# One planned order of a gated linear attention and token/channel mixer kernel against another: block 0's keys on VectorE, the rest planned anew

## The chip, the core and the metric

The kernel runs on one core of a Trainium2 chip, as one program. Five engines take instructions from queues of their own, each strictly in order: PE (TensorE, matrix products), DVE (VectorE), ACT (ScalarE), POOL (GpSimd) and SP (SyncE, which here only issues DMA transfers). They meet through semaphores. An instruction that is not ready holds up everything behind it on its engine. The metric is the device time of one execution in microseconds (us), the median of three runs; lower is better.

## What is computed

Two stages in a row. For each of 4 batches and 8 heads, a recurrence over 768 steps with a decaying 48 x 48 state; its output, as 768 x 384, goes through a mixer over tokens and then one over channels:

```python
# attention: q, k, v, alpha are (4, 8, 768, 48)
for t in range(768):
    state = alpha[:, :, t, :, None] * state + einsum('bhd,bhe->bhde', k[:, :, t], v[:, :, t])
    y[:, :, t] = einsum('bhd,bhde->bhe', q[:, :, t], state)
x = y.transpose(0, 2, 1, 3).reshape(4, 768, 384)
# mixer
h = maximum(x.transpose(0, 2, 1) @ w_tok1, 0) @ w_tok2      # 768 -> 256 -> 768
u = x + h.transpose(0, 2, 1)
out = u + maximum(u @ w_ch1, 0) @ w_ch2                     # 384 -> 1536 -> 384
```

Inputs and output are float32; the kernel multiplies in bfloat16.

## The kernel before

The sequence of each batch is cut into three chunks of 256 steps. Chunk n (0 to 11) belongs to batch n // 3. The 256 steps lie as 128 partitions x 2 slots, and the halves (hf 0 and 1) of a chunk are handled one after the other. The steps of a chunk, with the names that the program gives them (n behind the name):

- `ld_at`, `ld_qt`, `ld_kt`, `ld_vt`: loads of alpha, q, k, v, 384 KB each, issued from SP's queue or ACT's.
- `ln` (ACT, L598) takes the logarithm of alpha; `cumw` (PE, L604) sums it along the sequence; `E`, `Et`, `IE` (ACT, L637, L641) give the factor, the total and the inverse factor. From chunk 3 on a shorter form is used: `P`, `ln1`, `lnP` (L592, L595), `r`, `cum`, and `k0a`, `q0r` ahead of the scalings.
- `qq`/`ql` and `kk`/`kl` (L653): queries times E, keys times IE, one instruction for each slot in chunks 0 to 4; `vb` converts the values (L697 on ACT, L698 on DVE or POOL).
- `trq`/`trk` (PE, L666) transpose both, `evq`/`evk` copy the result out of PSUM. From chunk 6 on a DMA transpose does this (`dq`, `dk`, `pq`).
- `G` (PE): products of queries and keys; `mask` (DVE, L720) keeps the causal part. `K` (PE): products of keys and values; `s`, `sa`, `sm` make the new states; `vs`, `ka`, `kb`, `kc` are copies between partition halves.
- `ia`/`ib` and `y` (PE) give the output of a half, `x` copies it out.

The mixer of batch b has `t1` (PE, L805; chunk half kc of output block m) and its relu `ht`, `t2` (PE, L810) and the sum `u` (DVE, L814), the transposes `up` with copies `ut`, then `c1` (PE, L829: `c1_b_mc_half`, three products each) with its relu `rt` on ACT (L800) or DVE (L802), and `c2` (PE, L834) with `o` (DVE, L838) and the stores `st`. The weights are loaded in pieces (`ldw_wt10` and so on) and converted (`cw_...`). Mixer b runs on PE interleaved with the attention of batch b + 1.

Ahead of batch 0 there are fillers: `f1_...` and `f3_...` are one or three products of a tile of zeros (128 x 512) into a bank that the named step uses later. They compute nothing that is used. 28 such products are issued.

Nothing schedules this at run time. `build` (from L117) declares all steps with the engines that they may use. Three strings hold the plan: `ORDER` lists all 947 steps in the order of issue, each with a letter for its engine (t PE, s ACT, v DVE, g POOL, y SP); `BUFS` gives the buffer of each tile at its first use, PSUM banks among them; `GATES`, empty here, could tie transfers together. `run` reads them, and the last loop emits the steps one by one, so the order within an engine is the order in the string. The wait of a step comes from what it reads and from the former users of its buffers. One wait is added on top: `shared` (L684) makes steps with `port=True` (scalings, conversions, half copies on DVE and POOL) wait for the one before them in the list when that ran on the other of the two engines.

PSUM has 8 banks. A `c1` needs one until its `rt` has run; a `cumw`, a `K` or a `G` needs a pair.

Of the kernel before, what the change touches and what calls it, by code (L numbers as in the profile page):

```python
# [378 lines left out]
G0_0t sm1_0v f3_trq1t G1_0t K1t P3g ld_kt2y ld_vt2y lnP3s trk1t trq1t sa0_1t evk1s evq1s ld_kt3y qq2g mask0_0v  # L379
mask1_0v ldw_wt10y ld_vt3y sm0_1v cum3t y0_0t x0_0s ib0t sa1_1t f3_trq2t ld_at4y ld_qt3y ql2v trq2t sm1_1v kl2v E3s  # L380
IE3s kk2g vs0_1g ldw_wt11s y1_0t evq2v G0_1t ia1t kk3g f1_G11t ldw_wt20y ldw_wt21y mask0_1v k0a3g x1_0s G1_1t ld_kt4y
vb2s trk2t mask1_1v ldw_wc10y r13s ib1t K2t evk2s sa0_2t sm0_2v G0_2t cw_wt10s mask0_2v kl3g ldw_wc11y vs1_1g vs0_2g
vs1_2s ka3s vb3s f3_G12t G1_2t kb3s ldw_wc13y t1_0_1_0t y0_1t trk3t ld_at5y y1_1t cw_wt11g ib2t ia2t ln14s mask1_2v
y0_2t x0_1v x0_2v x1_1s vs1_3s vs0_3s ld_qt4s ldw_wc12y kc3g t1_0_1_1t y1_2t t1_0_0_0t t1_0_1_2t P4g t1_0_0_1t
t1_0_0_2t t1_0_0_3t t1_0_0_4t q0r3g x1_2v t1_0_0_5t t1_0_1_3t evk3v qq3g t1_0_1_4t ql3g lnP4s t1_0_1_5t k0a4g ht_0_0s
cw_wt20s K3t ht_0_1v cum4t cw_wt21s t2_0_0t t2_0_1t IE4s s0_3v sa1_3v u_0_0v t2_0_2t kk4g ldw_wc15y trq3t u_0_1v
u_0_2v t2_0_3t t2_0_5t kl4g E4s evq3s up_0_0t t2_0_4t u_0_3v cw_wc10s u_0_5v u_0_4v up_0_1t ut_0_1s ut_0_0v ld_vt4y
G1_3t G0_3t up_0_2t ib3t mask0_3v mask1_3v trk4t ldw_wc14y c1_0_0_0t c1_0_1_0t cw_wc11g ut_0_2s c1_0_2_0t c1_0_3_1t
r14s cw_wc13s ldw_wc21y c1_0_7_1t evk4s y1_3t y0_3t rt_0_1_0v q0r4v ka4v qq4v ql4g x0_3s x1_3v rt_0_0_0v rt_0_2_0v P5g
cw_wc15g c1_0_7_0t c1_0_6_1t rt_0_7_0s rt_0_7_1s cw_wc12s rt_0_3_1s c1_0_0_1t ld_qt5y c1_0_6_0t trq4t c1_0_2_1t  # L390
c1_0_4_1t ld_kt5y ldw_wc22y sm1_3g cw_wc14g vb4g lnP5s c1_0_10_1t evq4s ldw_wc20s rt_0_0_1s rt_0_6_0v rt_0_6_1v
ld_vt5s rt_0_2_1s c1_0_11_1t c1_0_11_0t rt_0_10_1v cum5t rt_0_11_1v G0_4t G1_4t kb4s IE5s rt_0_4_1v cw_wc21g kc4g
ln15s E5s c1_0_10_0t c1_0_3_0t r15s rt_0_10_0s c1_0_9_1t vs1_4g ldw_wc23y mask0_4v rt_0_9_1s rt_0_11_0s mask1_4v
ldw_wc24y c1_0_8_0t c1_0_4_0t c1_0_8_1t ia4t q0r5v vs0_4s y0_4t rt_0_8_0s rt_0_4_0s c1_0_1_1t c1_0_5_0t K4t c1_0_9_0t
ldw_wc25s rt_0_5_0s qq5v rt_0_8_1s x0_4s rt_0_9_0s cw_wc22s rt_0_3_0v rt_0_1_1v trq5t c1_0_5_1t ld_at6y k0a5g sa0_4v
# [36 lines left out]
c2_2_2_2t c2_2_1_1t t2_3_3t c2_2_2_3t o_2_3v u_3_5v c2_2_1_2t c2_2_1_3t u_3_4v o_2_4v u_3_3v c2_2_0_2t o_2_2v ux_3_1y
c1_3_7_0t c1_3_0_0t c1_3_4_0t c1_3_10_0t c1_3_5_0t c2_2_0_3t c1_3_2_0t rt_3_4_0s st_2_4s st_2_2y rt_3_5_0s rt_3_2_0s
# [459 lines left out]
```

## Time and profile before

| | us |
|---|---|
| median of three runs (lowest to highest) | 165.89 (165.33 to 166.85) |
| the profiled execution: its time | 165.84 |
| its span, first to last instruction | 164.1 |
| instructions in the span | 4068 |
| mean granted TensorE clock | 0.99 |

A row of the timeline has the start, the busy time, the engine, the line, the operation, the tiles written and read, their shapes and a count; in square brackets stands how long the engine had been idle before it and what ended that. A row of a group has the total busy time, the mean ns of one, and the idle time before the group with its releasers. PE is matrix products, PEld the loads of their stationary operand, which overlap. A matmul's end is modelled and includes its drain, so single durations are longer than the distance from one to the next. Engine names with q (ACTq, SPq) are issues of transfers.

### The profile page before, as it was taken

The numbers are of one execution on the slowest core, as the hardware profiler recorded it, in microseconds if no ns is written. First come the engines' busy times: TensorE is split into PE (matmuls) and PEld (weight loads), VectorE is DVE, ScalarE is ACT, GpSimd is POOL, SyncE is SP. The second block draws the span as 40 slices with busy tenths as digits, with TensorE's granted clock in tenths as the row PEclk, the third lists the DMA queues.
The fourth block names the chain that finished last, engine by engine and source line by source line (L and its number), as shares of the span: only waits on it lengthen the run. The fifth ranks groups of instructions, "written<-read, shape, count | busy, mean of one in ns | idle before, by whom it ended". The sixth has DMA issues, their size and how long they took to land.

```text
span 164.1 us, 4068 instructions
## 1 busy us (share of the span) xinstructions
PE 155.5 (95%) x1601; PEld 98.2 (60%) x1601; DVE 110.8 (68%) x197; ACT 101.1 (62%) x188; POOL 75.5 (46%) x94
## 2 busy tenths in 40 slices
PE   7959889899999999999999999999999999999992
PEld 2444656576657676665667666666566665566660
DVE  4056999689699777967789998874591283524341
ACT  3698798998998786289995947466615101562000
POOL 4054489972942827289795494739700000000000
PEclk9995999999999999999999999999999999999999
DMA  4999999999999998999999999699012135220314
GB/s 127 324 318 321 248 340 279 348 348 344 342 363 336 291 265 202 249 302 211 239 239 174 234 184 221 144 221 248 19 48 100 48 68 129 90 98 9 113 71 143
DMA packets 76322, 34.46 MB, mean 210 GB/s; under 512 B 68112, under 2 KB 76304, under 8 KB 76304
## 3 DMA queue, kind: packets, MB, share of 16 engines
q1 hardware_dynamic: 64704, 27.73, 66.5%
q10 hardware_dynamic: 11600, 6.49, 13.7%
q8 instruction: 12, 0.20, 0.5%
q14 instruction: 6, 0.05, 0.1%
HBM read 25.17 MB, written 4.72 MB: 182 GB/s over the span
## 4 chain that ended last, share of the span: by engine, by line
PE 52%; DVE 4%; ACT 2%; ACTq 1%; issue 1%
PE ps L834 22%; PE ps L829 19%; PE ps L604 6%; PE ps L805 3%; PE ps L810 2%; DVE u L814 1%; ACTq L545 1%; DVE o L838 1%; DVE pkk L653 1%; DVE ut L698 1%; ACT vb L697 0%; ACT ut L697 0%; DVE rt L802 0%; DVE ss L762 0%; ACT lf L592 0%
## 5 line engine op out<-in xcount | busy, mean ns | idle before, releaser
L834 PE MATMUL ps<-wc,rt 128*128 128x384 bf16 (+2 forms) x300 | 54.7, 320 | 0.0
L829 PE MATMUL ps<-ut,wc 128*128 128x384 bf16 x288 | 51.8, 326 | 0.3 <-ACT E L631 0.2
L800 ACT ACTIVATE rt<-ps 128x384 bf16<-128x384 f32 x55 | 25.3, 493 | 24.6 <-PE ps L829 24.5
L829 PEld LDWEIGHTS <-wc 128*128 128x128 bf16 x288 | 27.0, 98 | 17.7 <-issue 1.2
L834 PEld LDWEIGHTS <-rt 128*128 128x128 bf16 x300 | 27.6, 98 | 16.6
L802 DVE TENSOR_SCALAR rt<-ps 128x384 bf16<-128x384 f32 x41 | 21.6, 552 | 14.4 <-PE ps L829 13.9
L720 DVE TENSOR_TENSOR gtm<-ps,mk 128x1024 bf16<-128x1024 f32 x24 | 28.3, 1217 | 2.7 <-PE ps L604 2.5
L653 POOL TENSOR_TENSOR pkk<-in,IE 128x384 bf16<-128x384 f32 (+1 forms) x12 | 14.3, 1206 | 9.4 <-DVE pkq L653 6.3
L838 DVE TENSOR_TENSOR o<-ps,u 128x384 f32<-128x384 f32 (+2 forms) x25 | 13.3, 535 | 6.1 <-PE ps L834 6.0
L814 DVE TENSOR_TENSOR u<-ps,x 128x384 bf16<-128x384 f32 x24 | 12.3, 552 | 4.6 <-PE ps L810 4.5
L653 POOL TENSOR_TENSOR pkq<-in,E 128x384 bf16<-128x384 f32 (+1 forms) x8 | 11.2, 1408 | 7.0 <-DMA in<-in_moe_w_ch_dram 3.8
L697 ACT CAST x<-ps 128x384 bf16<-128x384 f32 x19 | 9.0, 481 | 7.7 <-PE ps L604 7.7
L697 ACT CAST vb<-in 64x384 bf16<-64x384 f32 (+1 forms) x18 | 11.8, 658 | 2.4 <-DMA in<-in_v_dram 1.6
L698 POOL CAST vb<-in 64x384 bf16<-64x384 f32 (+1 forms) x17 | 9.5, 559 | 7.0 <-issue 3.2
L805 PE MATMUL ps<-x,wt 128*128 128x384 bf16 x48 | 11.4, 326 | 0.3 <-ACT x L697 0.3
L604 PE MATMUL ps<-zs 128*128 128x512 bf16 x28 | 9.9, 495 | 1.1 <-DVE zs L507 1.1
L810 PE MATMUL ps<-ht,wt 128*128 128x384 bf16 x48 | 10.1, 326 | 0.7 <-ACT wt L697 0.7
L589 POOL TENSOR_TENSOR in<-in 128x384 f32<-128x384 f32 x9 | 9.0, 1000 | 3.4 <-DMA in<-in_alpha_dram 2.5
L653 DVE TENSOR_TENSOR pkq<-in,E 128x384 bf16<-128x384 f32 (+1 forms) x9 | 6.0, 689 | 6.5 <-ACT E L637 4.6
L645 POOL TENSOR_TENSOR in<-in,in 128x384 f32<-128x384 f32 x7 | 7.0, 1001 | 5.4 <-DVE in L649 3.0
L768 DVE TENSOR_TENSOR tmp<-ps,ss 128x384 f32<-128x384 f32 x12 | 6.6, 554 | 3.5 <-POOL ss L771 1.8
L604 PE MATMUL ps<-tpq,tpk 48*64 48x128 bf16 (+1 forms) x288 | 8.3, 221 | 0.3 <-ACT tpk L697 0.2
(93 smaller groups left out, 212.2 us busy)
## 6 DMA issues: line engine op xcount, KB each, us to landing
in<-in_alpha_dram SPq DMA_DIRECT2D x11, 384.0 KB, 6.3
in<-in_q_dram SPq DMA_DIRECT2D x10, 384.0 KB, 5.2
in<-in_moe_w_ch_dram SPq DMA_DIRECT2D x10, 384.0 KB, 7.3
in<-in_k_dram SPq DMA_DIRECT2D x9, 384.0 KB, 5.8
in<-in_v_dram SPq DMA_DIRECT2D x9, 384.0 KB, 6.0
out_dram<-o SPq DMA_DIRECT2D x14, 192.0 KB, 2.4
out_dram<-o ACTq DMA_DIRECT2D x9, 192.0 KB, 1.9
in<-in_moe_w_tok_dram SPq DMA_DIRECT2D x3, 384.0 KB, 5.6
```

Source lines behind the costliest of these rows:

```text
L604: return self.pe.matmul(out, lhsT=lhsT, rhs=rhs, start=start, stop=stop, skip_group_check=True)
L653: self.shared(self.eng[e].tensor_tensor(self.t(dst)[:, c : c + z, :, 0:D], self.t(src)[:, :, c : c + z, :].rearrange("p h s d -> p s h d") ...
L697: return self.act.copy(d, s)
L720: self.nc.vector.tensor_tensor(self.t(gtm)[:, hf, :, :], self.pair(gp).rearrange("p a (j t) -> p (a j) t", t=128), bass.AP(tensor=m.tensor ...
L800: self.act.activation(d, s, AF.Relu)
L802: self.nc.vector.tensor_scalar_max(d, s, 0.0)
L805: self.pe.matmul(self.bank(bank)[:, 0:HD], lhsT=self.wt1[:, kc, m * 128 : m * 128 + 128], rhs=self.t(x), start=(kc == 0), stop=(kc == NS - 1))
L810: self.pe.matmul(self.bank(bank)[:, 0:HD], lhsT=self.wt2[:, kc, i * 128 : i * 128 + 128], rhs=self.t(hts[kc]), start=(kc == 0), stop=(kc = ...
L814: self.nc.vector.tensor_tensor(self.t(u)[:, i % 3], self.bank(bank)[:, 0:HD], self.t(x), ALU.add)
L829: self.pe.matmul(self.bank(bank)[:, 0:HD], lhsT=self.wc1[:, kc, mc * 128 : mc * 128 + 128], rhs=self.t(ut)[:, 3 * half : 3 * half + 3, kc, ...
L834: self.pe.matmul(self.bank(bank)[:, 0 : cz - ca], lhsT=self.t(rts[mc][0])[:, i * 128 : i * 128 + 128], rhs=self.wc2[:, mc, ca:cz], start=( ...
L838: self.nc.vector.tensor_tensor(self.t(o)[:, ca:cz], self.bank(bank)[:, 0 : cz - ca], self.t(u)[:, i % 3, ca:cz], ALU.add)
```

## The change

Only `ORDER` and `BUFS` differ. No step is added or taken out but fillers: `f3_K0`, `f1_trq1`, `f3_trq1`, `f3_trq2`, `f1_G11` go and `f1_cumw1`, `f1_cumw2`, `f3_cumw2`, `f1_G01`, `f1_y2` come, so 24 products of zeros are issued instead of 28, 11 of them ahead of `cumw0` instead of 13.

In block 0, `kk0` and `kl0` move from POOL to DVE and `vb0` from ACT to DVE; `cumw1` comes ahead of `K0`, and `K0` ahead of `trk0`; `s0_0` comes ahead of `evq0`; `G0_0` and `mask0_0` come ahead of the products of block 1. `ld_vt0` and `ld_at1` are issued by ACT and not by SP, at the head of its queue. `evq1` moves from ACT to DVE, `ut_0_1` from ACT to DVE.

Over the whole kernel some 140 steps change their engine: 23 relus `rt` go from ACT to DVE and 20 the other way; ACT issues 21 loads and 14 stores where it issued 12 and 9; of the conversions of `w_ch1`/`w_ch2`, POOL keeps 3 of 6. Most PSUM banks and buffers are new. The order of each engine before and after, up to the first channel product:

```
before  PE   f3_trk0 f1_trq0 f3_trq0 f3_cumw1 f3_cumw0 cumw0 f1_K0 f3_K0 cumw1 trq0 trk0 K0 cumw2 sa1_0 f1_trq1 G0_0 ...
after   PE   f3_trq0 f3_cumw1 f1_trq0 f1_cumw1 f3_cumw0 cumw0 f1_cumw2 f3_trk0 f3_cumw2 f1_K0 trq0 cumw1 K0 trk0 sa1_0 cumw2 G0_0 ...
before  DVE  ql0 qq0 evq0 s0_0 qq1 ql1 sm1_0 mask0_0 mask1_0 sm0_1 ql2 sm1_1 kl2 evq2 mask0_1 mask1_1 sm0_2 mask0_2 mask1_2
             x0_1 x0_2 x1_2 evk3 ht_0_1 s0_3 sa1_3 u_0_0 u_0_1 u_0_2 u_0_3 u_0_5 u_0_4 ut_0_0
after   DVE  qq0 vb0 ql0 kl0 kk0 s0_0 evq0 sm1_0 mask0_0 qq1 ql1 mask1_0 evq1 sm0_1 ql2 qq2 mask0_1 x0_0 evq2 sm1_1 mask1_1
             sm0_2 mask0_2 mask1_2 x1_1 x1_2 evk3 ht_0_1 s0_3 sa1_3 u_0_1 u_0_2 u_0_0 u_0_3 u_0_5 u_0_4 ut_0_0 ut_0_1
before  POOL kk0 kl0 kk1 kl1 vs1_0 P3 qq2 kk2 vs0_1 kk3 k0a3 kl3 vs1_1 vs0_2 cw_wt11 ...
after   POOL kk1 kl1 P3 vs0_0 kk2 kl2 k0a3 kk3 vb3 kl3 vs1_3 kb3 P4 ka3 cw_wt11 ...
before  ACT  ln0 ln1 E0 IE0 IE1 Et0 vb0 E1 ln2 Et1 evk0 ... ht_0_0 cw_wt20 cw_wt21 IE4 E4 evq3 cw_wc10 ut_0_1 ut_0_2
after   ACT  ld_vt0 ld_at1 ln0 Et0 E0 IE0 ln1 ld_qt1 ln2 IE1 evk0 ... cw_wt20 ht_0_0 cw_wt21 IE4 E4 evq3 r14 cw_wc10 ut_0_2
```

The head of the diff:

```diff
 ORDER = """
-f3_trk0t f1_trq0t f3_trq0t f3_cumw1t f3_cumw0t ld_at0y ln0s ld_at1y ln1s ld_qt0y ld_kt0y ld_vt0y cumw0t E0s ql0v
-ld_at2y f1_K0t f3_K0t cumw1t qq0v trq0t ld_kt1y ld_vt1y IE0s IE1s evq0v ld_qt1y Et0s vb0s kk0g E1s ld_at3y kl0g trk0t
-ln2s Et1s evk0s K0t kk1g kl1g s0_0v cumw2t vb1s vs0_0s Et2s E2s IE2s ld_qt2y vs1_0g qq1v ql1v sa1_0t ln13s f1_trq1t
...
+f3_trq0t f3_cumw1t ld_vt0s f1_trq0t f1_cumw1t f3_cumw0t ld_at0y ld_at1s ln0s ld_qt0y cumw0t Et0s ld_kt0y ld_at2y
+ld_kt1y E0s IE0s ld_vt1y ln1s qq0v f1_cumw2t f3_trk0t f3_cumw2t ld_qt1s f1_K0t vb0v ln2s ld_at3y ql0v kl0v trq0t
+ld_qt2y kk0v cumw1t IE1s K0t trk0t kk1g evk0s s0_0v sa1_0t Et1s evq0v cumw2t kl1g sm1_0v G0_0t trk1t E1s Et2s vb1s
...
 BUFS = """
-3 0 4 1 11 1 13 0 5 3 11 2 0 0 1 6 0 1 2 0 0 17 0 0 9 1 0 1 2 0 1 0 1 16 0 0 2 4 0 6 0 4 7 1 3 3 1 6 1 0 5 2 1 5 2 1 6
...
+4 0 3 2 18 8 1 7 0 0 4 18 12 11 1 1 6 5 2 2 1 0 9 0 10 1 1 1 1 0 1 2 0 2 4 2 0 0 3 0 1 5 0 7 18 8 2 0 0 1 1 15 4 0 1 5
...
```

In the first channel stage, from `ut_0_2` to `lnP5`, ACT had `ut_0_2 r14 cw_wc13 evk4 x0_3 rt rt cw_wc12 rt lnP5` and now has `ut_0_2 ld_vt4 cw_wc13 evk4 rt rt rt rt ka4 rt rt ln15 rt ldw_wc22 ldw_wc23 lnP5`. PE had 14 `c1` ahead of `cum5` and now has 12, with `ib3` behind the first of them instead of ahead.

More of the change, by code (lines that the diff above doesn't have):

```diff
@@ L381 @@
[L381 to L395, printed above, removed]
@@ new lines @@
+sa0_8v x1_7s vs1_9s ld_at11s x0_7s x1_6s kb9s c2_1_0_0t c2_1_0_1t o_1_3v kc9s k0a10g G0_8t mask0_8v G1_8t sm0_8g
+t1_2_0_0t t1_2_1_0t c2_1_0_2t mask1_8v t1_2_0_1t ia8t t1_2_1_1t t1_2_1_2t t1_2_1_3t vs0_9s kk10g y0_8t K9t s0_9v
+t1_2_0_2t dk10y t1_2_0_3t pq9g ld_vt10y ib8t y1_8t x0_8s x1_8s c2_1_2_0t sa1_9v sm1_9v t1_2_0_4t t1_2_1_4t ld_kt11y
+t1_2_1_5t t1_2_0_5t G1_9t G0_9t ht_2_1v c2_1_2_1t c2_1_2_2t st_1_4s ln111s ht_2_0s pq10s mask1_9v ib9t P11g ka10g
+c2_1_2_3t kb10g t2_2_5t c2_1_0_3t mask0_9v u_2_5v t2_2_3t u_2_3v t2_2_4t u_2_4v y0_9t kc10g G0_10t y1_9t x0_9s lnP11s
@@ new lines @@
+o_1_2v t2_2_2t t2_2_0t mask0_10v c2_1_5_0t cum11t c2_1_5_1t ux_2_1y u_2_2v ia10t vb10g t2_2_1t ld_qt11y vs0_10g
+c2_1_5_2t x1_9s u_2_0v IE11s st_1_1s vs1_10s E11s r111s K10t y0_10t u_2_1v k0a11v c2_1_5_3t c1_2_3_1t ux_2_0y x0_10s
+c1_2_4_1t sa0_10v sm0_10v rt_2_3_1s c1_2_1_1t sa1_10v c1_2_0_1t kk11v c1_2_8_1t c1_2_10_1t rt_2_4_1s c1_2_5_1t
+c1_2_2_1t q0r11g rt_2_0_1s o_1_5v ld_vt11y rt_2_10_1s rt_2_8_1v c1_2_11_1t c1_2_9_1t qq11g st_1_3y rt_2_1_1v
+c1_2_10_0t rt_2_10_0s c1_2_11_0t rt_2_9_1v vb11s c1_2_7_0t c1_2_4_0t c1_2_6_1t rt_2_11_1v vs0_11s rt_2_5_1s rt_2_2_1v
@@ new lines @@
+c1_3_1_1t c1_3_3_1t rt_3_3_1v c1_3_10_1t c2_2_0_3t o_2_0v c1_3_11_0t rt_3_11_0v rt_3_6_1s c2_3_1_1t c1_3_2_1t
+c2_3_1_2t c1_3_4_1t c1_3_0_1t c1_3_9_1t rt_3_10_1s st_2_4s rt_3_2_1s st_2_2s c2_2_1_3t o_2_1v rt_3_9_1v rt_3_1_1s
+c1_3_7_1t c2_3_2_0t rt_3_0_1v rt_3_7_1s c2_3_0h0_0t c2_3_2_1t c1_3_8_1t c1_3_11_1t c1_3_9_0t rt_3_11_1s st_2_0s
+rt_3_8_1s c2_3_4_0t c1_3_5_1t c2_3_0h1_0t c2_3_2_2t c2_3_0h1_1t rt_3_9_0v c2_3_2_3t c2_3_3_0t c2_3_1_3t rt_3_5_1v
+rt_3_4_1v c2_3_4_1t o_3_2v st_3_2s c2_3_3_1t o_3_1v c2_3_4_2t c2_3_0h1_2t st_2_3s c2_3_4_3t st_2_1y c2_3_0h1_3t
```

96 lines of the change are left out of this document (48 added, 48 removed), and 20 rows, old and new, of the table BUFS.

## The prediction

> **What bounds the kernel now.** I read the page's totals first, then busy time in windows that I cut where the stages change, then the timeline of the start.
>
> ```profile
> PE 155.5 (95%) x1601; PEld 98.2 (60%) x1601; DVE 110.8 (68%) x197; ACT 101.1 (62%) x188; POOL 75.5 (46%) x94
> ```
>
> ```profile
> 0.00:36.28 36.28, 31.24 (x381) 19.18 (x382) 24.53 (x52) 29.45 (x47) 22.77 (x36) 0.95 1.03 294
> 36.28:44.10 7.82, 7.82 (x69) 4.87 (x67) 6.60 (x13) 7.12 (x13) 4.25 (x6) 1.00 1.12 341
> 72.00:160.90 88.90, 88.67 (x879) 55.76 (x877) 56.27 (x97) 44.27 (x90) 34.22 (x36) 1.00 0.63 143
> ```
>
> Columns: length, busy PE, weight loads, DVE, ACT, POOL, granted clock, DMA share, GB/s. PE (TensorE) idles 36.28 - 31.24 = 5.04 us before the first channel product (c1_0_0_0, at 36.28), and 0.00 and 0.23 us in the two later windows. So a new order can win only ahead of 36.28, and can lose anywhere. In 36.28:44.10 ACT is busy for 7.12 of 7.82 us and DVE for 6.60: extra work there finds little room.
>
> **The start, before.**
>
> ```profile
> 1.06 5.11 PE L604 MATMUL ps<-zs 128*128 128x512 bf16 x13 [1.06 <-DVE zs L507]
> 4.37 0.84 ACT L598 ACTIVATE la<-in 128x768 bf16<-128x768 f32 x1 [2.28 <-DMA in<-in_alpha_dram]
> 5.58 0.84 ACT L598 ACTIVATE la<-in 128x768 bf16<-128x768 f32 x1 [0.37 <-DMA in<-in_alpha_dram]
> 6.00 0.65 PE L604 MATMUL ps<-la,u 128*128 128x384 bf16 x3
> 7.06 0.81 ACT L637 ACTIVATE E<-ps 128x768 f32<-128x768 f32 x1 [0.64 <-PE ps L604]
> 7.91 1.03 DVE L653 TENSOR_TENSOR pkq<-in,E 128x384 bf16<-128x384 f32 x2 [4.57 <-ACT E L637]
> 9.08 1.96 POOL L653 TENSOR_TENSOR pkk<-in,IE 128x384 bf16<-128x384 f32 x2 [6.34 <-DVE pkq L653]
> 11.09 0.62 PE L666 MATMUL ps<-idn,pkk 128*128 128x128 bf16 x8 [1.70 <-POOL pkk L653]
> 11.64 0.52 PE L604 MATMUL ps<-vb,pkk 64*128 64x96 bf16 x16
> 11.82 1.96 POOL L653 TENSOR_TENSOR pkk<-in,IE 128x384 bf16<-128x384 f32 x2 [0.79 <-DMA in<-in_k_dram]
> 12.26 0.56 DVE L762 TENSOR_TENSOR ss<-ps,E 128x384 bf16<-128x384 f32 x1 [1.53 <-PE ps L604]
> ```
>
> Chunk 0's keys take 1.96 us on POOL and PE waits 1.70 us for them; K0 comes at 11.64, the first state (s0_0) at 12.26. The seventh load (kt1) is there at 11.82, the first at 4.37: one load each (11.82 - 4.37) / 6 = 1.24 us.
>
> **Part 1, the first loads and fillers.** Eleven fillers stand ahead of cumw0 instead of 13: 0.42 us less (estimate: one spacing of 5.11 / 13, as the last are shorter), so cumw0 at about 5.55 and E0, behind the short Et0, at 6.75 to 7.55; IE0 to 8.35. vt0 and at1 now go out on ACT's queue beside qt0 and kt0 on SP's. The same five loads land first, by 4.37 + 4 x 1.24 = 9.3 us, but at1 and kt0 are now the last of them (5.58 and about 8.1 before). If SP's are served first, kt0 lands at about 8.1. DVE then does qq0, vb0, ql0 until 9.2 (0.52 each by the row of 7.91; vb0 put at the same) and kl0, kk0 (1.03) until 10.2 to 10.4. cumw1 now stands ahead of K0 on PE, and needs ln1 (0.84 us behind IE0 and at1: done by 9.2 to 10.15). So K0 runs at 10.8 to 11.2 and s0_0 at 11.3 to 11.7; I take 11.5, 0.75 us ahead of 12.26.
>
> The Trainium skill (DMA: Bandwidth & Descriptors, Issuing engines are not separate DMA queues) says that transfers of all issuing engines run on the same 16 DMA engines and interleave. By that rule the later end, 11.7, holds and the sum would be 0.2 us longer. The trace of before, with its early loads on one queue, cannot show it.
>
> **Part 2, DVE becomes the chain from there.** These forms come up:
>
> ```profile
> 15.79 2.34 DVE L720 TENSOR_TENSOR gtm<-ps,mk 128x1024 bf16<-128x1024 f32 x2
> L762 DVE TENSOR_TENSOR ss<-ps,E 128x384 bf16<-128x384 f32 x8 | 4.4, 552 | 2.1 <-PE ps L604 2.1
> L698 DVE COPY tpq<-ps 128x1024 bf16<-128x1024 bf16 x2 | 2.6, 1315 | 0.7 <-PE ps L666 0.7
> L653 POOL TENSOR_TENSOR pkk<-in,IE 128x384 bf16<-128x384 f32 x9 | 8.9, 1003 | 9.4 <-DVE pkq L653 6.3 <-PE ps L666 1.8 <-DMA in<-in_k_dram 1.2
> L698 POOL CAST vb<-in 64x384 bf16<-64x384 f32 x14 | 7.0, 501 | 4.3 <-issue 3.2 <-DVE pkk L698 0.4
> ```
>
> and the stage ended so:
>
> ```profile
> 26.86 1.48 DVE L698 CAST x<-ps 128x384 bf16<-128x384 f32 x3
> 26.87 0.82 POOL L698 CAST wt<-in 128x768 bf16<-128x768 f32 x1
> 28.07 0.46 ACT L697 CAST x<-ps 128x384 bf16<-128x384 f32 x1
> 28.58 1.14 PE L805 MATMUL ps<-x,wt 128*128 128x384 bf16 x6 [0.34 <-ACT x L697]
> 30.04 0.47 ACT L800 ACTIVATE ht<-ps 128x384 bf16<-128x384 f32 x1
> 31.29 1.15 PE L810 MATMUL ps<-ht,wt 128*128 128x384 bf16 x6 [0.67 <-ACT wt L697]
> 31.82 1.49 DVE L814 TENSOR_TENSOR u<-ps,x 128x384 bf16<-128x384 f32 x3 [0.39 <-PE ps L810]
> 36.28 2.69 PE L829 MATMUL ps<-ut,wc 128*128 128x384 bf16 x15
> ```
>
> From s0_0 to the last x (x1_2) the new order puts on DVE five states (5 x 0.552 = 2.76), three evq (3 x 1.315 = 3.95; evq0 was done earlier and evq1 was ACT's), six masks (6 x 1.17 = 7.02), four query scalings (2.06) and three x (1.48): 17.3 us. Before, the same stretch took 26.86 + 1.48 - 12.26 = 16.1. From 11.5 it ends at 28.8. In one place DVE must wait: G0_2 stands behind y1_1, which needs mask1_1; only sm0_2 covers that, some 0.4 us stay open (estimate, by the like wait of 0.39 in the row of 31.82). So 29.2, where the last x was done at 28.53. POOL agrees: kk2 waits for qq2 on DVE (8.7 us of the list behind s0_0, at 20.2), then come six 1.00 us products, vb3 (as the cast of 26.87), three half copies (0.50) and cw_wt11 (0.82): 9.15 us, to 29.35. Before, that weight was ready at 27.69. The six products that need both start at 29.4, 0.8 behind 28.58.
>
> **Part 3, to the first channel product.** Before, the ht were done at 30.51 and PE waited 0.67 us for wt2's cast, until 31.29. Now cw_wt20 stands ahead of ht_0_0, so that wait goes and the next thing, the late ht (31.3), takes its place: 31.4, 0.1 late. But on DVE s0_3 and sa1_3, then six u (0.50 each) and now both ut_0_0 and ut_0_1 stand in one line behind ht_0_1:
>
> ```profile
> L698 DVE COPY ut<-ps 128x768 bf16<-128x768 bf16 x3 | 1.6, 550 | 0.0
> ```
>
> 31.3 + 2 x 0.55 + 6 x 0.5 + 2 x 0.55 = 36.5; with the small waits for PE shown at 31.82 (0.39) 36.9. c1_0_0_0 starts 0.6 us late.
>
> **Part 4, the channel stage.** Between ut_0_2 and lnP5, which cum5 waits for, ACT now has ut_0_2, three DMA issues, cw_wc13, evk4, seven relus (rt), ka4, ln15 and lnP5; before it had three relus there and no issue.
>
> ```profile
> L697 ACT COPY ut<-ps 128x768 bf16<-128x768 bf16 x3 | 2.4, 793 | 0.2 <-PE ps L821 0.2
> L697 ACT CAST wc<-in 128x768 bf16<-128x768 f32 x5 | 4.2, 832 | 0.0
> L697 ACT COPY tpk<-ps 128x1024 bf16<-128x1024 bf16 x4 | 4.1, 1024 | 0.0
> L800 ACT ACTIVATE rt<-ps 128x384 bf16<-128x384 f32 x55 | 25.3, 493 | 24.6 <-PE ps L829 24.5
> L697 ACT COPY kt<-pkk 64x384 bf16<-64x384 bf16 x7 | 3.6, 508 | 0.5 <-POOL pkk L653 0.4
> L595 ACT ACTIVATE la<-in 128x384 bf16<-128x384 f32 x9 | 4.7, 520 | 0.7 <-POOL in L589 0.6
> 42.36 0.46 ACTq L545 DMA_DIRECT2D in<-in_v_dram  x1
> 44.10 0.33 PE L604 MATMUL ps<-la,u 128*128 128x384 bf16 x1
> 107.81 9.27 PE ps L829 x57
> ```
>
> 0.79 + 3 x 0.40 + 0.83 + 1.02 + 7 x 0.49 + 0.51 + 2 x 0.52 = 8.8 us. ut_0_2 cannot start before 36.3, so lnP5 ends at 45.1 and cum5 comes at 45.2, not 44.10. Ahead of cum5 PE has 12 channel products of 3 x 9.27 / 57 = 0.49 us where it had 14 (ib3, 0.17 us, has moved in). So PE is 1.1 + 2 x 0.49 - 0.17 = 1.9 us behind there: 0.6 from the start, the rest idle, partly as banks wait for relus. Behind this PE had no idle that could give it back. Later stages are reordered with 35 transfers issued by ACT instead of 21 (9 more loads, 5 more stores); at 0.4 us each ACT has room after 72 us (44.27 of 88.90 busy). I cost them at nothing, with 0 to 2.5 us as bounds. Fillers removed later (15 to 13) stand where DVE is the chain: nothing.
>
> Sum: the profiled execution's own 165.84 us (span 164.1) + 1.9 = 167.7; the median of the runs, 165.89, is the same within 0.05. I take 167.8.
>
> **Rivals.** (a) The gain at the start comes through. If DVE's chain is shorter than counted and the weights are early, the 0.75 us of s0_0 survives, and of the 5.04 us of idle ahead of 36.28 about 1.5 us more goes: 163.6. For it: the 1.70 us wait goes, K0 no longer waits for POOL. Against: 17.3 us of DVE work behind it. Chance 0.18. (b) The two cancel: c1_0_0_0 at 36.3, and cum5's producers are in time as ACT's relus are taken up in waits: 165.9. Chance 0.22. (c) ACT's issues stall. An issue that takes as long as a whole load, 1.24 us, holds the relus queued behind it; it decides once three of the seven issues around the first channel stage do so: 2.5 us on top of the 1.9, 170.2. Against: the row of 42.36 took 0.46. Chance 0.15.
>
> **How the numbers follow.** About 1% (1.66 us) is what a measurement of this kernel can tell from no change; it lies at 164.2 and 167.55. The forecast, delays of 0.6 us at c1_0_0_0 and 1.3 at cum5, has a chance of 0.45. Its own range is 166.9 to 168.9 (s0_0 0.2 earlier or later, the 0.4 and 0.39 us of waits there or not, up to 0.4 of later idle), so 0.31 of it is slower by over 1% and 0.14 within. Rival (a) gives 0.15 faster and 0.03 within, (b) 0.22 within, (c) 0.15 slower. Together: faster 0.15, same 0.39, slower 0.46. For 8 in 10 the range leaves out the faster half of (a), 0.09, and the half of (c), 0.08, that lies above 170: 164.0 to 170.0.
>
> **What would show it.** Right, if in the new profile the two scalings of block 0 run on DVE from about 9.3 us and its first state near 11.5; if DVE is busy with hardly a gap from there to the last x, which ends near 29.2; if the cast of wt on POOL ends near 29.3, the first L829 product stands near 36.9, and PE waits about a microsecond for the ACT line L595 a few microseconds behind it, at 45. Wrong, if DVE shows gaps of more than a microsecond between 12 and 29 (then another engine or a load is the chain), if L829 begins before 36.3, if PE shows no wait between 37 and 46, or if PE idles after 72 us, which I cost at nothing: a wait there, for late loads or transposes, would add to the sum.

## The result and the profile after

| | us |
|---|---|
| median after, 20 executions (lowest to highest) | 166.62 (166.06 to 167.45) |
| median before, 20 executions beside them | 165.61 (165.02 to 166.85) |
| ratio after to before, 95% interval | 1.0063 (1.0045 to 1.0080) |
| profiled execution after: time, span | 167.07, 165.3 |

The change makes the kernel 1.0 us slower, where 1.9 were forecast: the right direction, half the size. Each ratio here and below leaves disturbed executions out and can differ from the quotient of the two medians by a few tenths of a per cent. The profiled execution lies 0.45 above its median; the one before lay 0.05 below its own.

The windows of after, cut at its own first channel product and its own cum5, with the columns of those before (length, PE, weight loads, DVE, ACT, POOL, granted clock, DMA share, GB/s):

```profile
0.00:37.23 37.23, 31.36 (x373) 19.54 (x374) 27.14 (x57) 26.51 (x44) 21.70 (x36) 0.95 1.05 305
37.23:44.38 7.15, 7.10 (x68) 4.51 (x66) 7.09 (x10) 6.80 (x14) 2.56 (x4) 1.00 1.08 324
72.00:162.06 90.06, 89.77 (x887) 56.65 (x884) 60.71 (x103) 42.39 (x86) 33.32 (x35) 1.00 0.58 135
```

The first stretch is 0.95 us longer than before (37.23 against 36.28). Behind it PE idles 0.05 us up to cum5, and 0.29 us behind 72. The chains of both kernels end in the last `o`, and its start is when the last product is done. First after, then before:

```profile
162.06 0.49 DVE o L838
```

```profile
160.90 0.49 DVE o L838
```

That is 1.16 us: the 0.95 of the first channel product, 0.17 for ib3, which before stood ahead of that product and now stands behind it, and 0.04. So in these two profiles the whole loss arises ahead of the first channel product. Behind it a few tenths say little: from the first channel product to that `o` before takes 124.62 us and after 124.83, and the profiles of twelve edits of after reach from 124.4 to 125.0.

The timeline of after, with the rows that answer to the start and to the mixer before:

```profile
5.07 0.84 ACT L598 ACTIVATE la<-in 128x768 bf16<-128x768 f32 x1 [2.99 <-DMA in<-in_alpha_dram]
5.96 0.65 PE L604 MATMUL ps<-la,u 128*128 128x384 bf16 x3
9.35 1.02 DVE L653 TENSOR_TENSOR pkk<-in,IE 128x384 bf16<-128x384 f32 x2
11.45 0.56 DVE L762 TENSOR_TENSOR ss<-ps,E 128x384 bf16<-128x384 f32 x1 [1.08 <-PE ps L604]
20.43 1.96 POOL L653 TENSOR_TENSOR pkk<-in,IE 128x384 bf16<-128x384 f32 x2 [2.85 <-PE ps L604]
...
28.88 0.82 POOL L698 CAST wt<-in 128x768 bf16<-128x768 f32 x1
28.93 0.56 DVE L698 CAST x<-ps 128x384 bf16<-128x384 f32 x1 [0.53 <-PE ps L604]
29.76 1.15 PE L805 MATMUL ps<-x,wt 128*128 128x384 bf16 x6 [0.54 <-POOL wt L698]
29.77 0.50 POOL L698 COPY pkk<-pkk 64x384 bf16<-64x384 bf16 x1
30.35 1.00 POOL L653 TENSOR_TENSOR pkq<-in,E 128x384 bf16<-128x384 f32 x1
31.31 1.00 POOL L649 TENSOR_TENSOR in<-in,lf 128x384 f32<-128x384 f32 x1
31.84 1.14 PE L810 MATMUL ps<-ht,wt 128*128 128x384 bf16 x6 [0.32 <-ACT ht L800]
32.39 1.00 POOL L653 TENSOR_TENSOR pkq<-in,E 128x384 bf16<-128x384 f32 x1
33.44 0.62 PE L666 MATMUL ps<-idn,pkq 128*128 128x128 bf16 x8 [0.46 <-POOL pkq L653]
```

Block 0's keys are on DVE, and the first state comes 0.81 us sooner (11.45 against 12.26). At the mixer's first stage that lead is gone: the six products wait for POOL's cast of the weight, 29.76 against 28.58. Behind that cast POOL still has a copy (kc3) and three 1.00 us products to do before ql3 is there, and PE waits for ql3 a second time, at 33.44. Before, ql3 was done at 32.22 and PE did not wait for it. The first of the two is the larger: the six products are 1.18 us late, and from them to the first channel product after takes 7.47 us, where before took 7.70 with ib3's 0.17 in it.

The granted clock in windows of 1 us after (the columns of the windows above):

```profile
13.00:14.00 1.00, 0.64 (x18) 0.46 (x14) 0.89 (x3) 0.89 (x4) 1.00 (x2) 1.00 1.17 324
14.00:15.00 1.00, 0.78 (x9) 0.55 (x10) 1.00 (x2) 0.83 (x1) 0.01 (x1) 1.00 1.22 339
15.00:16.00 1.00, 0.38 (x8) 0.21 (x7) 1.00 (x4) 0.48 (x1) 0.00 (x0) 0.93 1.11 307
16.00:17.00 1.00, 1.00 (x10) 0.80 (x12) 1.00 (x1) 1.00 (x2) 0.98 (x1) 0.50 1.18 319
```

PE is given half its clock from 15.9 to 19.3, where before the same came from 12.2 to 15.6. That was the first suspect.

### The profile page after: what moved, and what is told of

Read it like the earlier page. It is cut to its first block, busy times and chain, and to the rows that moved or that the text cites. A ratio compares the mean times of both kernels' runs of the same rounds, so it can differ in the third digit from the quotient of the medians.

```text
span 165.3 us, 4045 instructions
## 1 busy us (share of the span) xinstructions
PE 155.8 (94%) x1597; PEld 98.8 (60%) x1597; DVE 116.7 (71%) x206; ACT 96.7 (59%) x182; POOL 76.8 (46%) x91
## 4 chain that ended last, share of the span: by engine, by line
PE 76%; DMA 9%; POOL 7%; ACT 2%; DVE 2%; SPq 1%; issue 1%; POOLq 0%; DVEq 0%
PE ps L834 27%; PE ps L829 27%; PE ps L604 12%; DMA in<-in_v_dram 4%; PE ps L805 4%; PE ps L810 4%; DMA out_dram<-o 3%; DMA in<-in_alpha_dram 3%; POOL pkk L653 2%; PE ps L666 2%; POOL pkq L653 1%; PE ps L821 1%; SPq L545 1%; ACT tpq L697 1%; DVE o L838 1%
## 5 line engine op out<-in xcount | busy, mean ns | idle before, releaser
L800 ACT ACTIVATE rt<-ps 128x384 bf16<-128x384 f32 x52 | 23.8, 491 | 30.9 <-PE ps L829 29.3
L802 DVE TENSOR_SCALAR rt<-ps 128x384 bf16<-128x384 f32 x44 | 23.1, 552 | 11.0 <-PE ps L829 11.0
L653 POOL TENSOR_TENSOR pkk<-in,IE 128x384 bf16<-128x384 f32 (+1 forms) x13 | 17.0, 1316 | 17.5 <-DVE ss L762 9.3
L697 ACT CAST vb<-in 64x384 bf16<-64x384 f32 (+1 forms) x23 | 14.3, 622 | 0.5 <-DMA in<-in_v_dram 0.2
L589 POOL TENSOR_TENSOR in<-in 128x384 f32<-128x384 f32 x8 | 8.0, 1001 | 9.6 <-DVE pkq L653 6.6
L649 POOL TENSOR_TENSOR in<-in,lf 128x384 f32<-128x384 f32 x9 | 9.0, 1000 | 6.0 <-DVE pkk L653 4.7
L653 POOL TENSOR_TENSOR pkq<-in,E 128x768 bf16<-128x768 f32 (+1 forms) x7 | 11.1, 1581 | 1.1 <-PE ps L829 0.7
L697 ACT CAST x<-ps 128x384 bf16<-128x384 f32 x16 | 7.5, 476 | 6.5 <-PE ps L604 4.0
L604 PE MATMUL ps<-zs 128*128 128x512 bf16 x24 | 8.6, 501 | 1.2 <-DVE zs L507 1.1
L604 PE MATMUL ps<-vb,gtm 128*128 128x48 bf16 x192 | 7.9, 183 | 0.2
```

Of the source, the lines that this page charges most:

```text
L604: return self.pe.matmul(out, lhsT=lhsT, rhs=rhs, start=start, stop=stop, skip_group_check=True)
L653: self.shared(self.eng[e].tensor_tensor(self.t(dst)[:, c : c + z, :, 0:D], self.t(src)[:, :, c : c + z, :].rearrange("p h s d -> p s h d") ...
L697: return self.act.copy(d, s)
L800: self.act.activation(d, s, AF.Relu)
L802: self.nc.vector.tensor_scalar_max(d, s, 0.0)
```

## The experiments

Only the order, the engines and the fillers are edited. The diffs show the list `ORDER`; BUFS follows. Each time is a median, with the ratio to the kernel before on the same chip.

**GpSimd's third block of keys sooner.**

```diff
-sm0_1v ql2v qq2v ld_vt3y vs1_1s cum3t ib0t G0_1t ld_at4y ld_qt3y mask0_1v kk2g kl2g
+sm0_1v kk2g ql2v qq2v ld_vt3y vs1_1s cum3t ib0t G0_1t ld_at4y ld_qt3y mask0_1v kl2g
```

> The changed kernel with one step moved in the list: kk2 (POOL) ahead of ql2 and qq2 (DVE), so that POOL need not wait for qq2 by the port order. Theory P (the loss is POOL's unbroken work from 20.43 to 33.39 us, which holds cw_wt11 and so the t1 products, and ql3 and so trq3): kk2 starts near 18.0, the rest of POOL's list comes 1.0 us earlier, cw_wt11 ends near 28.7, c1_0_0_0 starts near 36.7 instead of 37.2, the time falls by 0.4 to 0.6 us. Theory D (as predicted: DVE's list up to the last x sets the end): the last x stays near 29.5, the time within 0.2 us.

Measured 166.94, ratio 1.0060 (1.0029 to 1.0091): nothing gained. kk2 started at 18.95 instead of 20.43, but the added port turn made DVE wait for it, and the cast of the weight ended only 0.31 us sooner (29.39). The row of DVE in this kernel:

```profile
19.99 1.03 DVE L653 TENSOR_TENSOR pkq<-in,E 128x384 bf16<-128x384 f32 x2 [1.28 <-POOL pkk L653]
```

**No filling at 27 us.**

```diff
-G0_2t f3_G12t G1_2t
+G0_2t G1_2t
```

> The changed kernel without the three products of zeros ahead of G1_2 (f3_G12), 0.65 us of PE time at 25.5 us. Theory D, with PE in DVE's chain: y1_2 and the last x come 0.5 us earlier, the time falls by 0.4 us. Theory P: cw_wt11 still ends at 29.7 and holds the t1 products; the time within 0.2 us. If the fillers keep the clock up, the granted clock falls below 1.00 after 26 us and the time rises.

Measured 166.51, ratio 1.0064 (1.0040 to 1.0088): no gain in the median. The profiled execution had the full clock throughout; in it the first channel product started at 36.74, and the wait for ql3 was 0.40.

**Block 0's keys alone, in the kernel before.**

```diff
-IE1s evq0v ld_qt1y Et0s vb0s kk0g E1s ld_at3y kl0g trk0t
+IE1s kk0v kl0v evq0v ld_qt1y Et0s vb0s E1s ld_at3y trk0t
```

> The kernel before with only block 0's two key scalings on DVE, ahead of evq0. Both theories: the keys are ready near 10.0 instead of 11.04, trk0 starts near 10.1 instead of 11.1 and s0_0 near 11.3 instead of 12.3. If the new place of these scalings is what costs (DVE more loaded by 1.03 us), the time rises by 0.3 to 1.0 us. If they are harmless by themselves and the loss lies in the rest of the new order, the time stays within 0.3 us of before; if the start is what counts, it falls by up to 0.7 us.

Measured 165.89, ratio 1.0025 (0.9993 to 1.0056). This is the named edit of the change, and it brings nothing by itself. The first state comes at 10.77 instead of 12.26, and then DVE stands still:

```profile
10.77 0.56 DVE L762 TENSOR_TENSOR ss<-ps,E 128x384 bf16<-128x384 f32 x1
14.39 1.03 DVE L653 TENSOR_TENSOR pkq<-in,E 128x384 bf16<-128x384 f32 x2 [3.06 <-POOL vb L698]
```

The next query scaling starts at 14.39; before, it started at 14.38. It takes its turn of the port behind POOL's steps, and POOL cannot begin them sooner, since they wait for chunk 1's keys to land:

```profile
11.84 1.95 POOL L653 TENSOR_TENSOR pkk<-in,IE 128x384 bf16<-128x384 f32 x2 [9.11 <-DMA in<-in_k_dram]
13.86 0.50 POOL L698 CAST vb<-in 64x384 bf16<-64x384 f32 x1
```

**Four more issues on ACT.**

```diff
-ldw_wc21y ... ld_qt5y ... ld_kt5y ... ldw_wc20y
+ldw_wc21s ... ld_qt5s ... ld_kt5s ... ldw_wc20s
```

> The changed kernel with four more loads issued by ACT and not by SP between ut_0_2 and lnP5 (wc21, qt5, kt5, wc20): seven issues there instead of three. As priced in the prediction, 0.40 us of ACT time each: lnP5 comes 1.6 us later, cum5 1 us later or more, the time rises by about 1.3 us. Rival: an issue runs beside the ACT work ahead of it and costs ACT next to nothing: relus start as before, the time within 0.3 us. A third outcome: an issue waits for its buffer or for the queue and holds ACT for over a microsecond at once.

Measured 173.83, ratio 1.0486 (1.0438 to 1.0535). The issues were not free here, and then one held ACT and so PE:

```profile
37.14 1.19 ACTq L569 DMA_DIRECT2D in<-in_moe_w_ch_dram  x1
38.37 0.83 ACT L697 CAST wc<-in 128x768 bf16<-128x768 f32 x1 [0.99 <-POOL in L649]
```

```profile
42.57 1.50 SPq L545 DMA_DIRECT2D in<-in_alpha_dram  x2
51.15 0.37 ACTq L569 DMA_DIRECT2D in<-in_moe_w_ch_dram  x1
51.62 0.87 ACT L800 ACTIVATE rt<-ps 128x384 bf16<-128x384 f32 x2 [3.17 <-DVE pkq L653]
52.16 1.05 PE L829 MATMUL ps<-ut,wc 128*128 128x384 bf16 x3 [3.41 <-ACT rt L800]
```

lnP5 started at 44.15, 7.32 us behind the first channel product at 36.83; in after it is 43.60 - 37.23 = 6.37. The four issues cost 0.95 us there, not 1.6, and most of it is one: the first, of wc21, took 1.19 us, and the conversion behind it started 0.04 us after its end, with ACT idle for 0.99. The releaser in the row had been done at 37.58.

The second hold, of 3.17 us, is at the issue of wc24, which after has on ACT too. Its buffer had been free since POOL's conversion of wc14 ended at 43.92. What it waited for was a landing. Every load tells its landing by one of eight semaphores, and in the trace an issue waits until the load that used its semaphore last has landed. For wc24 that was the first of SP's two alpha loads of the row at 42.57, which landed at 51.07.

So rival (c) of the prediction is real: the issue of 1.19 us is close to the 1.24 us that it named. After itself has one hold ahead of cum5, of 1.30 us, and there it is a buffer in use (shown with the copy kc3 below).

**Copies back to ACT, first loads back, and both.** In turn:

```diff
-vs1_3g ... kb3g ... ka3g
+vs1_3s ... kb3s ... ka3s
```

```diff
-ld_vt0s ... ld_at0y ld_at1s ln0s ld_qt0y cumw0t Et0s ld_kt0y ... vb0v ... kk0v
+ld_at0y ld_at1y ln0s ld_qt0y cumw0t Et0s ld_kt0y ld_vt0y ... kk0v vb0v
```

> The changed kernel with three half copies of chunk 3 (vs1_3, kb3, ka3) on ACT, where they were before, and not on POOL ahead of cw_wt11. Theory P (POOL's list from kk2 to ql3 holds the start stage): POOL is 1.5 us shorter there, cw_wt11 ends near 28.2 instead of 29.7, PE's wait for trq3 (0.46 us) goes, and what is late next is the last x at 29.5: c1_0_0_0 0.3 to 0.6 us earlier, the time 0.3 to 0.6 us less. Theory L (the start is paced by the loads of chunks 1 to 4 and by the order of PE, and each engine's list fits around them): within 0.2 us.

> The changed kernel with the first five loads as before (at0, at1, qt0, kt0, vt0, all from SP) and vb0 behind kk0 on DVE. ln0 starts at 4.4 instead of 5.07, cumw0 near 5.5, the keys of block 0 are ready near 9.6 instead of 10.4 and s0_0 starts near 10.7 instead of 11.45. If the first 12 us set the end, the time falls by 0.5 to 0.7 us. If the wait for chunk 1's data takes the gain back (as DVE's start on chunk 1's queries at 14.4 did in the kernel before, whether its keys ran on DVE or POOL), it stays within 0.2 us.

> The changed kernel with the two edits above (half copies on ACT, first loads as before) and without the three products of zeros ahead of G1_2. Theory P: together 0.8 to 1.2 us less, c1_0_0_0 near 36.2, the time that of the kernel before within 0.3 us. Theory L: no more than 0.4 us less.

Measured 167.51 (1.0118, 1.0085 to 1.0152), 168.24 (1.0140, 1.0099 to 1.0182) and 168.36 (1.0173, 1.0133 to 1.0214); the third has both edits and no filling at 27 us. All lose. With the copies on ACT, POOL's cast of the weight ended at 27.70 and PE no longer waited for ql3, but ACT was late instead (PE waited 0.48 us for a copy of x and 0.30 for a weight cast of ACT's). With the first loads as before, the first state came at 10.67, but then ACT stood for the third alpha:

```profile
12.42 0.84 ACT L598 ACTIVATE la<-in 128x768 bf16<-128x768 f32 x1 [3.62 <-DMA in<-in_alpha_dram]
```

So the earlier first state brings nothing here; as the edit adds a wait of its own, it does not show what ACT's early issues cost by themselves. In both, PE was granted half its clock for longer (17.0 to 23.9, and 15.3 to 25.6), which is why the clock stayed a suspect.

**No fillings in the second block, in the kernel before.**

```diff
-f1_trq1t G0_0t sm1_0v f3_trq1t G1_0t
+G0_0t sm1_0v G1_0t
```

> The kernel before without the four products of zeros ahead of trq1 (f1_trq1, f3_trq1), behind which G0_0 and G1_0 ran at half clock until 16.0 us. If they delayed the stage, G1_0 comes near 15.3 and the time falls by 0.3 to 0.6 us, below both kernels. If other waits cover them, within 0.2 us; if they kept the clock up, the granted clock is low for longer than 12 to 16 us and the time rises.

Measured 166.02, ratio 1.0028 (0.9999 to 1.0056). The half-clock stretch lasted 6.8 us instead of 3.4, and the time moved by 0.3% (by the interval at most 0.6%).

**The clock itself.** Products of zeros into the sparse stretch, in after and then in before:

```diff
-G0_0t trk1t ... G1_0t ... trq1t K1t ... f1_G01t
+G0_0t f1_trk1t trk1t ... G1_0t ... f1_trq1t f1_K1t trq1t K1t
```

```diff
-f1_K0t f3_K0t cumw1t qq0v trq0t ... trk0t ... f1_trq1t G0_0t sm1_0v f3_trq1t G1_0t
+cumw1t qq0v trq0t ... f1_trk0t f3_K0t f1_K0t trk0t ... G0_0t sm1_0v G1_0t
```

> The kernel after, with three single products on zeros put into TensorE's sparse stretch from 13.2 to 16.0 us (one ahead of the second key transposes, two ahead of the second query transposes) and one taken out behind them. Theory 1, the half-clock stretch that follows there makes the loss: it goes, the first channel product starts at 36.8 and the time is 166.2. Theory 2, the loss is in the order of the work and a half-clock stretch costs at most 0.3 us of the total, as the after runs at granted clock 1.00 (166.45) against those at 0.99 (166.86) say: the time stays at 166.4 or above.

> The kernel before, with three of its fillings (one ahead of K0, two ahead of the second query transposes) put into TensorE's gap from 9.4 to 11.1 us and four products on zeros left out at 13.8 to 16.0. Theory 1: no half-clock stretch at 12.3, the first products of block 0 come up to 1 us sooner, and the time falls by 0.3 to 0.6, to 165.2. Theory 2: DVE still waits for chunk 1's values to 14.4, the loads set the pace, and the time stays within 0.2 of before.

Measured 166.55 (1.0039, 1.0015 to 1.0063) and 166.17 (1.0032, 0.9997 to 1.0067): no gain is shown. In after the median stays (166.55 against 166.62); the ratio is 0.24% lower, but the intervals overlap. Sorting the executions by their mean granted clock says more. Of after, 7 of 20 had 1.00, with a median of 166.45; with the added products 7 of 12 had it, with 166.48. Of the kernel before, 14 of the 125 executions beside the experiments had 1.00, with 165.36, and 12 had 0.996 to 0.999, with 165.90. In the one profile at 0.996 (of the edit of the kernel before that comes next) the clock drops only behind 162 us; if these 12 are taken with the first group on that account, the 26 have 165.73. At the full clock the two kernels are 0.7 to 1.1 us apart, about as far as in all executions, so the half-clock stretch does not make the loss. What it costs is less clear: the 9 of after at 0.99 had 166.86, about 0.4 us more, but the 3 at 0.977, with more time at the half clock, had 166.57.

**Block 0's keys and a later transpose of block 4's, in the kernel before.**

```diff
-evq0v ... kk0g ... kl0g ... trk4t ldw_wc14y c1_0_0_0t ... c1_0_3_1t
+kk0v kl0v evq0v ... ldw_wc14y c1_0_0_0t ... c1_0_3_1t trk4t
```

> The kernel before with block 0's two key scalings on VectorE, as in the earlier run of that edit alone, and block 4's key transposes moved behind the first four channel products. In the earlier run the second token product started 0.41 us sooner than before (30.88) and TensorE then waited 1.18 us for those keys. If that wait is all that took the gain back, the first channel product starts at 35.8 instead of 36.28 and the time is 165.3 (0.3 to 0.5 below before). Rival: the weights of the channel products or block 4's work is late next, and the time stays within 0.2 of before.

Measured 166.02, ratio 1.0000 (0.9964 to 1.0036): the rival. The first channel product started at 35.94, but with block 4's transposes (0.45 us from one to the next) still to come, so PE stood where it stood before.

**GpSimd's list behind the weight: a scaling to DVE.** Three tries; the first puts qq3 behind x1_1, the second behind x1_2 with ql3 behind it, the third is the second without the filling at 27 us:

```diff
-qq3g q0r3g ql3g t1_0_1_1t x0_2s x1_1v y1_2t
+q0r3g ql3g t1_0_1_1t x0_2s x1_1v qq3v y1_2t
```

```diff
-qq3g q0r3g ql3g t1_0_1_1t x0_2s x1_1v y1_2t ldw_wc10y t1_0_0_2t x1_2v
+q0r3g t1_0_1_1t x0_2s x1_1v y1_2t ldw_wc10y t1_0_0_2t x1_2v qq3v ql3g
```

> The kernel after, with block 3's scaled queries qq3 made by VectorE behind x1_1, in its 0.5 us wait, and not by GpSimd. Theory 2, GpSimd's list behind cw_wt11 holds the query transposes of block 3: ql3 ends 1.0 us earlier, the wait of 0.46 at 33.44 goes, the first channel product starts 0.4 earlier than in the kernel after (36.8) and the time is 166.2. Rival: the key work of block 4 or the second half of the token-mixing weights is late next, and the time stays at 166.6.

> The kernel after, with block 3's scaled queries qq3 made by VectorE behind x1_2 and GpSimd's ql3 issued behind it, so that VectorE does not wait for ql3 as it did in the run before. Theory 2, a step of GpSimd's list holds TensorE at the transposes of block 3's queries: ql3 ends near 32.0 instead of 33.4, the wait of 0.46 at 33.44 goes, and the time is 0.4 under that of the kernel after, 166.2. Rival: the next late step takes the wait, and the time stays at 166.6.

> The same, without the three products on zeros at 27 us. If the two costs are separate and each holds TensorE, the time is 0.3 under the first of the two, 165.9, which leaves 0.3 to 0.5 of the loss against before; if the gains do not add, it is within 0.1 of it.

Measured 170.50 (1.0272, 1.0230 to 1.0313), 167.61 (1.0117, 1.0081 to 1.0153) and 167.97 (1.0142, 1.0111 to 1.0173). None tests the theory, since each edit adds a wait of its own. On DVE, first try and then second:

```profile
32.28 0.56 DVE L653 TENSOR_TENSOR pkq<-in,E 128x384 bf16<-128x384 f32 x1 [3.88 <-POOL pkq L653]
```

```profile
31.42 0.56 DVE L653 TENSOR_TENSOR pkq<-in,E 128x384 bf16<-128x384 f32 x1 [1.94 <-POOL in L649]
```

qq3 takes its turn of the port behind the POOL step that stands ahead of it in the list, and the x, the state and the u behind it on DVE wait with it. Moving one instruction that takes 0.56 us on DVE and 1.00 on POOL cost 1 to 4 us.

**The same list shortened without a port turn.** kc3, a copy of 0.50 us, goes to ACT, which in after stands there for 1.30 us at the issue of wc13, until POOL's cast frees its buffer:

```profile
29.74 0.37 ACTq L567 DMA_DIRECT2D in<-in_moe_w_ch_dram  x1
30.16 0.52 ACT L595 ACTIVATE la<-in 128x384 bf16<-128x384 f32 x1 [1.30 <-POOL wt L698]
```

The second kernel has no filling at 27 us either.

```diff
-cw_wt11g ldw_wc11y G0_2t f3_G12t G1_2t trk3t kc3g ... ldw_wc13s lnP4s
+cw_wt11g ldw_wc11y G0_2t f3_G12t G1_2t trk3t ... kc3s ldw_wc13s lnP4s
```

> The kernel after, with the copy kc3 (0.50 us at 29.77) taken from GpSimd's list and given to ScalarE, ahead of the transfer at which it stands from 28.9 to 30.2. It needs no turn of the port. Theory 2, GpSimd's list behind cw_wt11 holds TensorE at block 3's query transposes: ql3 ends at 32.8 instead of 33.4, the wait of 0.46 at 33.44 goes, the first channel product starts 0.4 sooner (36.8) and the time is 166.2. Rival: another step takes the wait and the time stays within 0.15 of 166.6.

> The same, without the three products on zeros at 27 us. If both costs hold TensorE one after the other, the first channel product starts at 36.4, as in the kernel before, and the time is 165.8 to 165.9; if they are one cost, the time is that of the run with kc3 alone or of the one without the products (166.5).

Measured 166.65 (1.0047, 1.0015 to 1.0080) with kc3 alone and 166.10 (1.0015, 0.9987 to 1.0043) with both. The first one's timeline:

```profile
28.37 0.82 POOL L698 CAST wt<-in 128x768 bf16<-128x768 f32 x1
29.16 1.00 POOL L653 TENSOR_TENSOR pkq<-in,E 128x384 bf16<-128x384 f32 x1
29.25 1.15 PE L805 MATMUL ps<-x,wt 128*128 128x384 bf16 x6 [0.19 <-POOL wt L698]
...
31.20 1.00 POOL L653 TENSOR_TENSOR pkq<-in,E 128x384 bf16<-128x384 f32 x1
31.33 1.14 PE L810 MATMUL ps<-ht,wt 128*128 128x384 bf16 x6 [0.32 <-ACT ht L800]
32.30 0.61 PE L666 MATMUL ps<-idn,pkq 128*128 128x128 bf16 x8
36.10 2.11 PE L829 MATMUL ps<-ut,wc 128*128 128x384 bf16 x12
```

ql3 ends at 32.20, 1.19 us sooner than after (0.51 of it since POOL's cast started at 28.37 already, in a profile at the full clock), and the wait of PE for it is gone: from the second token product (31.33) to the first channel product takes 4.77 us, where after takes 37.23 - 31.84 = 5.39 and the run without the filling, also at the full clock, 36.74 - 31.41 = 5.33. The time does not clearly follow: the median is no better, and the 5 of 12 executions at the full clock have 165.82 against 166.45 after, but they reach from 165.63 to 167.39. With both edits the loss against before is gone within the interval, which lies wholly, if barely, below that of after (1.0045 to 1.0080).

**Both, and the products of zeros in the sparse stretch.** This is the last kernel with the three single products of the clock experiment.

> The kernel after with kc3 on ScalarE, without the three products on zeros at 27 us, and with the three single products of the earlier run put into TensorE's sparse stretch from 13.2 to 16.0 us (7 of its 12 executions had a granted clock of 1.00, against 7 of 20 of the kernel after). If the half-clock stretches are what is left of the loss in the run with kc3 and without the filling, the median falls from 166.1 to the 165.9 that its executions at granted clock 1.00 had, at most to 165.5, the level of the kernel before. If they are not, or if the products themselves delay the first chunks, it stays at 166.1 or above.

Measured 165.98, ratio 1.0024 (0.9998 to 1.0050). The profiled execution had the full clock, and its first channel product at 36.23. It differs from the run without them by less than the intervals. Here the clock does not sort the executions: the 4 at 1.00 have a median of 166.20, the 6 below 0.99 one of 165.80. So this run gives no sign that the half-clock stretches are what is left. None of the kernels came below the one before by more than its interval.

## Where the prediction held and where it failed

**Part 1 held.** The first state was put at 11.5 and came at 11.45. That it came so close is partly luck, as several terms were off and cancelled. ln0 came at 5.07, not at 4.37: SP issued at0 at 0.81 us and ACT vt0 at 0.83, and at0 landed 0.7 us later than before. So cumw0 was at 5.96 and not at 5.55, and kt0 landed at 9.22, not at about 8.1. The Trainium skill (DMA: Bandwidth & Descriptors, Issuing engines are not separate DMA queues) says that transfers of all issuers interleave; these two landings agree, but the first state did not move to the 11.7 that the prediction tied to that rule. The fillers saved 5.11 - 4.79 = 0.32 us, not 0.42 (and 5.11 / 13 is 0.39). The keys on DVE ran from 9.35 to 10.37, as said.

**Part 2 held within 0.35 us.** DVE shows no gap above 0.54 between the first state and the last x, which ended at 29.49 (29.2 said); kk2 started at 20.43 (20.2) and POOL's cast ended at 29.70 (29.35); the six products started at 29.76 (29.4).

**Part 3 had the length, by another path.** The first channel product came 0.95 us late, not 0.6, but the difference came in with the six products. From them to the channel product the prediction has 36.9 - 29.4 = 7.5 us and the trace 7.47. The part took DVE's list as the chain, with 0.39 us of waits, and ql3 to be in time. It did not follow POOL's list past the cast of the weight, though it had the row of 1.00 us for each of the three products behind it: 29.70 + 0.50 + 3 x 1.00, with the gaps between them, is the 33.39 at which ql3 ended. PE waited 0.46 us for it, and DVE then 0.57 for PE, ahead of the sums u at 34.75. With kc3 on ACT the first of these waits is gone and the same stretch takes 36.10 - 29.25 = 6.85 us, so that 7.5 came out was luck.

**Part 4 is the step that failed.** It took ACT's list for the chain, with a price for each issue, put ACT's work from ut_0_2 to lnP5 at 8.8 us and cum5 at 45.2, with PE idle for most of 1.3 us. ACT needed 7.1 us, cum5 ran at 44.38, and PE idled 0.05: that PE shows no wait between 37 and 46 was one of the prediction's own signs of being wrong. ACT and its queue in after:

```profile
36.99 0.80 ACT L697 COPY ut<-ps 128x768 bf16<-128x768 bf16 x1 [0.47 <-PE ps L821]
37.07 0.39 ACTq L545 DMA_DIRECT2D in<-in_v_dram  x1
37.68 0.83 ACT L697 CAST wc<-in 128x768 bf16<-128x768 f32 x1
38.42 1.02 ACT L697 COPY tpk<-ps 128x1024 bf16<-128x1024 bf16 x1
39.32 0.89 ACT L800 ACTIVATE rt<-ps 128x384 bf16<-128x384 f32 x2
...
41.26 0.51 ACT L697 COPY kt<-pkk 64x384 bf16<-64x384 bf16 x1
41.32 0.38 ACTq L569 DMA_DIRECT2D in<-in_moe_w_ch_dram  x1
41.67 0.48 ACT L800 ACTIVATE rt<-ps 128x384 bf16<-128x384 f32 x1
41.74 0.48 ACTq L569 DMA_DIRECT2D in<-in_moe_w_ch_dram  x1
42.06 0.47 ACT L800 ACTIVATE rt<-ps 128x384 bf16<-128x384 f32 x1
42.55 0.52 ACT L592 ACTIVATE lf<-in 128x384 f32<-128x384 f32 x1
42.98 0.47 ACT L800 ACTIVATE rt<-ps 128x384 bf16<-128x384 f32 x1
43.60 0.52 ACT L595 ACTIVATE la<-in 128x384 bf16<-128x384 f32 x1 [0.15 <-POOL in L589]
44.38 0.33 PE L604 MATMUL ps<-la,u 128*128 128x384 bf16 x1
```

None of the three issues delayed an instruction of ACT. The first starts inside ut_0_2, which stands ahead of it in the list. The other two, of wc22 and wc23, start at 41.32 and 41.74, although ln15 (42.55) and a relu (42.98) stand ahead of them in the list: the queue was ahead of the compute. So the 3 x 0.40 of the sum were worth nothing here. Two relus in a row advance 0.44 to 0.45 us each and not the 0.49 that one lasts. And the lnP5 that was held to follow ACT's list last waited for POOL (0.15). By the prediction's own count PE was 44.38 - 44.10 + 2 x 0.49 - 0.17 = 1.09 us behind at cum5, so part 4 cost 0.14 and not 1.3. That an issue costs nothing is not a rule: the run with four more has one that cost 0.99.

**Later stages at nothing:** right. **Rivals:** (a) did not come; (b), with the first channel product at 36.3, is what the list with kc3 on ACT comes near; (c) is what the run with four more issues shows; in after one issue held ACT, for 1.30 us ahead of the second token product, where PE then waited 0.32. The named edit, block 0's keys on DVE, shows neither a gain nor a loss in the kernel before (1.0025); that the loss is a by-product of the new order behind it is argued from there.

What stays open is how the 1.0 us divides. The 1.18 us by which the six token products are late behind POOL's cast was never taken away by an edit that added no wait: kc3 stands behind that cast in POOL's list, and the filling is work of PE. At the full clock the kernel without the filling had 166.11 (4 executions), with kc3 on ACT 165.82 (5), with both 165.92 (6), which is too few to say whether the two add; in the medians only both together show. And at the full clock 0.2 to 0.6 us (165.92 against 165.73 or 165.36) are unexplained.

## What to carry to other kernels

A wait removed at the start is worth what the next list on each engine leaves of it: follow every engine's list to the next point at which TensorE needs its result, not only that of the engine that got more work. Where instructions of two engines take turns in the order of a list, one moved to the faster engine waits for all that the other has ahead of it; take a step that needs no turn. Before a clock or a stall is blamed, sort the executions by it: two kernels that differ as much at the same clock differ for another reason.

## What the runs showed of the hardware

An issue of a transfer on ACT took 0.38 to 0.48 us in the first channel stage of after and none of ACT's compute; two of the three began over 1.2 us ahead of an instruction that stands before them in the list. It can cost: one of 1.19 us kept ACT's compute idle for 0.99. An issue whose buffer was in use held ACT for 1.30 us, and one that had to wait for an earlier load to land, 3.17 us.

In before and after TensorE's granted clock fell to a half without an idle time above 1.70 us: after the gap of 1.70 us before 11.09 in the kernel before, and after three microseconds at 0.64, 0.78 and 0.38 busy in after. It stayed so for 3.4 us; in other runs for 6.8 (the run without fillings in the second block) or 10.2 (the one with the first loads back), and executions of one kernel differed in it (7 of 20 of after had none). The Trainium skill (TensorE: Matmul & The Clock Gate, What's actually happening) has a free-running window of about 3.4 us, with which the lengths and the differences between executions agree, and half the clock after an idle window of that length. Such an idle time stands in one profile alone, the 3.41 us with four more issues, and half the clock followed it for 3.4 us; the other stretches came without one.
